# Side work moved to other units of a Fourier stage, and three output loads issued two units later, in a one-core kernel

## The chip, the cores and the metric

The kernel runs on one core of one Trainium2 chip. The metric is device time in microseconds (us) of one execution: the median of several runs.

## The reference

The inputs are `x` (2048 x 640), two pairs of Fourier matrices (real and imaginary, 2048 x 2048 and 640 x 640), `W_gate` and `W_up` (640 x 1728) and `W_down` (1728 x 640), all in fp32.

```python
xn   = layernorm(x)
a, b = xn @ hid_re.T, xn @ hid_im.T
y    = seq_re @ a - seq_im @ b                      # the Fourier mix
h    = relu(xn @ W_gate) * (xn @ W_up)
out  = x + y + h @ W_down
```

## The kernel before

Every matrix product is made in three matmuls of type fp32r (`mm3`, lines 129 to 131): each operand is split into a high and a low part, the high one by ScalarE (line 123), the low one by VectorE as the difference (line 124), and high x high, high x low and low x high are added up in PSUM. On top of that the 2 x 2 block products are made in Winograd's way, with seven products instead of eight, named B11, B21, T1, T2, B22, T3, T4. The T products need differences of blocks, which VectorE makes first (line 605 in the Fourier stage, 1060 in the last one).

Three stages follow each other.

1. The Fourier stage over the sequence. It runs over four chunks c of 512 output tokens. A chunk's products are cut into four units each (g = 0 to 3); a unit loads a 128 x 1024 tile of the Fourier matrix (`raw`, six buffers), splits it into a tile `cb` (a ring of three buffers) and runs 12 matmuls, or 18 for units of T1 and B22. A chunk from the second on is T1 x4, then T2 and B22 mixed, then T3 x4, then T4 x4. When a product's last unit is done, `combine` reads its sums out of PSUM with VectorE (lines 503, 506, 587).
2. The gate and up product (`gate_up`), first for the second pair of chunks (q = 1: tokens 1024 to 2047), then for the first.
3. The last stage (`project`), for q = 1 and then q = 0: it multiplies the Fourier result by the hidden Fourier matrices and `h` by `W_down`, seven products of six units each.

Stages 1 and 3 are written as a list `todo` of units, each with a load, a prepare, a run and a finish step. `drive(4, 2)` walks through the list: at place i it issues the load of unit i, the splits of unit i - 2, the matmuls of unit i - 4 and the finish of unit i - 5. In stage 1 this is the program's order, which a scheduler still changes by its own estimates; in stage 3 it holds as written on SyncE's and GpSimd's queues (SP and POOL).

Two kinds of side work stand in the list.

- Token steps: stage 2 needs blocks of normalized, transposed tokens of pair q = 1, with sums of them. Six steps (`token_sets`) make them. The first two (light) take two VectorE operations of 128 x 512 (lines 359, 360). The other four (heavy) take four of 128 x 512 (lines 378, 379) and four of 128 x 256 (line 385). Such a step is a list entry with no matmul of its own: at its place it loads `st` tiles (a pool of two buffers) from POOL's queue, six places later its VectorE work is made, and eight places later its stores to `set` are issued from POOL's queue. Chunk 3 then loads the nine finished sets on SP's queue (`K` and `A`, line 679) and splits them (`r` and `xs_early`).
- Loads of `y`: the output tiles begin as a piece of x, loaded on SP's queue (`get_y`, line 1161) after the fourth unit of a product, and the product's sums are added to them at its end (line 1164).

In the list before, the entry V3 stands at place 43. A token step is placed two entries after it, and each further one at least nine entries after the one before:

```python
            if n == "V3":
                free[0] = len(todo) + 2
            if free[0] is not None and len(todo) >= free[0] and steps:
                token_sets(*steps.pop(0))
                free[0] = len(todo) + SPACE
```

The loads of stage 3 are `rw` (data, line 1019 from the Fourier stage, 1021 from the stage of the gate) and `wr` (weights, lines 1050 to 1054); their splits are `cb` and `wt`.

Of the kernel before, what the change touches and what calls it, by code (L numbers as in the profile page):

```python
# [35 lines left out]
B11, B12, B21, B22, T1, T2, T3, T4, X4 = range(9)  # L36
# [22 lines left out]
def fnet_reglu_kernel(  # L59
# [84 lines left out]
    todo = []  # L144
# [270 lines left out]
    def sums_124(g):  # L415


        def make():
            both = lambda g, cs: [xn_block(g, cs, v) for v in range(2)]
            a11, a21, a12, a22 = both(g, K1), both(g, K2), both(g + NH, K1), both(g + NH, K2)  # L420
            s1, s2 = (i.rearrange("p (j d) -> p j d", j=SG) for i in (lambda t: (t[:, :CH], t[:, CH:]))(stage()))
            w = s4_part(g)
            tt = nc.vector.tensor_tensor
            f = lambda i: i.bitcast(F32)
            tc.keep_in_program_order(tt(s1, f(a21[0]), f(a22[0]), op=OP.add))
            tt(s1, s1, f(a22[1]), op=OP.add)
            tt(s2, s1, f(a11[0]), op=OP.subtract)
            tt(s2, s2, f(a11[1]), op=OP.subtract)
            split(*a21, s1)

            tt(s1, f(a12[0]), s2, op=OP.subtract)
            tt(s1, s1, f(a12[1]), op=OP.add)
            split(*a11, s2)
            split(w[:, :, 0], w[:, :, 1], s1)

        todo.append((idle, make, idle, idle))

    def sums_3(g):


        def make():
            s = stage()[:, :CH].rearrange("p (j d) -> p j d", j=SG)
            tt = nc.vector.tensor_tensor
            a22, s2 = ([xn_block(n, cs, v).bitcast(F32) for v in range(2)] for n, cs in ((g + NH, K2), (g, K1)))
            tc.keep_in_program_order(tt(s, a22[0], s2[0], op=OP.subtract))
            tt(s, s, a22[1], op=OP.add)
            tt(s, s, s2[1], op=OP.subtract)
            split(xn_block(g + NH, K1, 0), xn_block(g + NH, K1, 1), s)

        todo.append((idle, make, idle, idle))  # L450
# [220 lines left out]
    def load_set(q, blocks, get=stage):  # L671
        t = {}

        def load():
            if "sets_b" not in late:
                late["sets_b"] = {1: get_r1(F32R)}
            for i in blocks:
                t[i] = get()
                nc.sync.dma_start(t[i], sets[q][i])

        def prepare():
            for i in blocks:
                split(*set_parts(q, i), t[i])

        return load, prepare, idle, idle
# [15 lines left out]

    steps = [(q, i) for q in (1,) for i in range(SET_STEPS)]
    early_sets, first_sets = list(SETS_A), list(SETS_B)
    free, splits = [None], []
    SPACE = 9

    def phase(c, names):


        for n in names.split():  # L710
            if n == "K":
                later = load_set(1, [first_sets.pop(0)])
                todo.append((later[0], idle, idle, idle))
                splits.append((idle, later[1], idle, idle))
            elif n == "A":
                later = load_set(1, [early_sets.pop(0)])
                todo.append((later[0], idle, idle, idle))
                splits.append((idle, later[1], idle, idle))
            elif n == "s":
                todo.append(splits.pop(0))  # L720
            elif n[0] == "W":
                sums_124(int(n[1]))
            elif n[0] == "V":
                sums_3(int(n[1]))
            elif n[0] == "B" and n[2] == "1":
                first_stream(int(n[3]), n[:3], int(n[4]))
            else:
                stream(c, n[:-1], int(n[-1]))
            if n == "V3":
                free[0] = len(todo) + 2  # L730
            if free[0] is not None and len(todo) >= free[0] and steps:
                token_sets(*steps.pop(0))
                free[0] = len(todo) + SPACE

    for n in ("B11", "B21"):
        for g in range(NH):
            phase(0, f"{n}0{g} {n}1{g}")
    phase(0, "B1120 B1130 B1121 B1131 W0 B1122 B1132 B1123 W1 B1133 B2120 B2130 W2 B2121 B2131 B2122 V0 W3 B2132 B2123 B2133")
    phase(0, "V1 T10 T11 V2 T12 T13 V3 T20 B220 T21 B221 T22 T23 B222 B223 T30 T31 T32 T33 T40 T41 T42 T43")
    for c in range(1, NCHUNK - 1):  # L740
        phase(c, "T10 T11 T12 T13 T20 B220 T21 B221 T22 T23 B222 B223 T30 T31 T32 T33 T40 T41 T42 T43")
# [267 lines left out]
    def project(q):  # L1009
# [135 lines left out]
        def plain_run(tiles):  # L1145
            for key, e, c in tiles:
                new = key not in B
                if new:
                    B[key] = bank()
                cs, es = slice(c * CH, (c + 1) * CH), slice(PLACE[e] * P, (PLACE[e] + 1) * P)  # L1150
                (w, wr), (h, hr) = (PW["w"], PW["wr"]), (plain["h"], plain["hr"])
                mm3(B[key], (w[:, 0, es], w[:, 1, es]), (h[:, 0, cs], h[:, 1, cs]), new, False, not new)
                for v in range(2):
                    nc.tensor.matmul(B[key], wr[:, v, es], hr[:, cs], start=False, stop=v == 1, skip_group_check=not new)  # L1154

        def get_y(name):

            for e, c in {"B11": ((0, 0), (1, 0), (4, 1)), "T1": ((2, 1), (3, 1)), "B21": ((4, 0),),
                         "T2": ((0, 1), (1, 1)), "T4": ((2, 0), (3, 0))}.get(name, ()):
                y[e, c] = t = pool("y").tile([P, CH], F32, name=f"y{e}{c}")  # L1160
                nc.sync.dma_start(t, xt[e * P : (e + 1) * P, (c0 + c) * CH : (c0 + c + 1) * CH])  # L1161
# [28 lines left out]
        def read(name):  # L1190
            for r in reading(name):
                add_y(*r)

        for name in ("B11", "T1", "B21", "T2", "B22", "T3", "T4"):

            tiles = {"B21": [(("c", i), i, 0) for i in range(2)] + [("v1", 4, 0)],
                     "B22": [(("b", i), i, 1) for i in range(2)] + [("v2", 4, 1)],
                     "T3": [(("o", i), 2 + i, 1) for i in range(2)]}.get(name)
            for u in range(len(units)):
                l, p, r = unit(name, u, u == 0)  # L1200
                end = u == len(units) - 1 and not (tiles and name != "T3")
                todo.append((l, p, r, (lambda name: lambda: read(name))(name) if end else idle))
                if u == 3:
                    todo.append(((lambda name: lambda: get_y(name))(name), idle, idle, idle))
                if name == "B21" and u in (0, 2):
                    (plain_rest if u else plain_block)()
            if tiles:
                todo.append((idle, idle, (lambda t: lambda: plain_run(t))(tiles),
                             (lambda n: lambda: read(n))("own" if name == "T3" else name)))
            if name == "T3":  # L1210
                todo.append((idle, idle, lambda: plain_run([(("a", i), 2 + i, 0) for i in range(2)]), idle))

    PW, PARTS = {}, {"T2": Z2, "T3": Z3, "T4": Y22}
    for q in (1, 0):
        project(q)
# [41 lines left out]
```

## Time and profile before

| | us |
|---|---|
| median of 3 runs | 1036.84 |
| lowest, highest of them | 1034.75, 1037.27 |
| time of the profiled execution | 1032.92 |
| its span, first to last instruction | 1031.2 |
| TensorE (PE) busy | 1022.8 |
| VectorE (DVE) busy | 800.9 |
| ScalarE (ACT) busy | 433.3 |
| GpSimd (POOL) busy | 96.6 |

The profile is one execution; times in it count from its first instruction. A row of the timeline gives start, duration, engine, line, operation, output<-inputs, shape and count, and in brackets the idle time before it with what ended that. Matmul durations overlap, so for PE the distance from start to start is what counts. A row of the windows gives a stretch, its length, and then for PE, PEld (weight loads), DVE, ACT and POOL the busy time and the number of instructions; after them the granted clock, the share of the DMA engines' time and GB/s.

### The profile page before, as it was taken

The numbers are of one execution on the slowest core, as the hardware profiler recorded it, in microseconds if no ns is written. First come the engines' busy times: TensorE is split into PE (matmuls) and PEld (weight loads), VectorE is DVE, ScalarE is ACT, GpSimd is POOL, SyncE is SP. The second block draws the span as 40 slices with busy tenths as digits, with TensorE's granted clock in tenths as the row PEclk, the third lists the DMA queues.
The fourth block names the chain that finished last, engine by engine and source line by source line (L and its number), as shares of the span: only waits on it lengthen the run. The fifth ranks groups of instructions, "written<-read, shape, count | busy, mean of one in ns | idle before, by whom it ended". The sixth has DMA issues, their size and how long they took to land.

```text
span 1031.2 us, 12409 instructions
## 1 busy us (share of the span) xinstructions
PE 1022.8 (99%) x4528; PEld 844.3 (82%) x4528; DVE 800.9 (78%) x1072; ACT 433.3 (42%) x543; POOL 96.6 (9%) x161
## 2 busy tenths in 40 slices
PE   8999999999999999999999999999999999999998
PEld 7888888888888888888888888888888888888886
DVE  7947986978979897688878988886597667886764
ACT  6754443333333543333335443443355423552531
POOL 2000010101211001321110000000000000000000
PEclk9999999999999999999999999999999999999999
DMA  7975744957968864863364665654599647986543
GB/s 301 370 241 163 259 157 143 312 209 254 326 195 298 314 206 153 273 227 133 142 250 143 225 235 215 226 224 156 178 350 296 193 129 225 373 304 222 156 153 122
DMA packets 100156, 233.29 MB, mean 226 GB/s; under 512 B 11392, under 2 KB 50816, under 8 KB 98688
## 3 DMA queue, kind: packets, MB, share of 16 engines
q1 hardware_dynamic: 83088, 163.82, 47.4%
q0 software_dynamic: 17008, 68.69, 18.4%
q8 instruction: 35, 0.57, 0.2%
q14 instruction: 25, 0.20, 0.1%
HBM read 177.41 MB, written 54.02 MB: 224 GB/s over the span
## 4 chain that ended last, share of the span: by engine, by line
PE 96%; DVE 2%; issue 1%; DMA 1%; POOL 0%; SPq 0%; ACT 0%; POOLq 0%; DVEq 0%; ACTq 0%
PE ps L131 31%; PE ps L130 31%; PE ps L129 31%; PE ps L1154 1%; DMA rw<-hd 1%; DVE cb L124 0%; PE ps L493 0%; PE ps L465 0%; POOL cb L289 0%; DVE tk L605 0%; DVE raw L605 0%; DVE st L385 0%; DVE st L378 0%; SPq L1161 0%; DVE st L379 0%
## 5 line engine op out<-in xcount | busy, mean ns | idle before, releaser
L131 PE MATMUL ps<-cb,wt 128*128 128x512 f32 x390 | 151.9, 390 | 0.4 <-DVE wt L124 0.4
L129 PE MATMUL ps<-cb,wt 128*128 128x512 f32 x390 | 151.9, 390 | 0.0
L130 PE MATMUL ps<-cb,wt 128*128 128x512 f32 x390 | 151.8, 389 | 0.0
L124 DVE TENSOR_TENSOR cb<-rw,cb 128x1024 fp32r<-128x1024 f32 x83 | 94.0, 1133 | 68.6 <-ACT cb L123 67.9
L123 ACT ACTIVATE cb<-rw 128x1024 fp32r<-128x1024 f32 x83 | 82.0, 987 | 147.9 <-PE ps L131 127.2
L123 ACT ACTIVATE cb<-raw 128x1024 fp32r<-128x1024 f32 x78 | 82.5, 1059 | 123.5 <-PE ps L131 101.8
L124 DVE TENSOR_TENSOR cb<-raw,cb 128x1024 fp32r<-128x1024 f32 x78 | 95.2, 1221 | 38.9 <-ACT cb L123 38.6
L131 PE MATMUL ps<-xs_early,gw 128*128 128x512 f32 x260 | 101.2, 389 | 0.0
L130 PE MATMUL ps<-xs_early,gw 128*128 128x512 f32 x260 | 101.2, 389 | 0.0
L129 PE MATMUL ps<-xs_early,gw 128*128 128x512 f32 x260 | 101.1, 389 | 0.0
L130 PE MATMUL ps<-cb,xs_late 128*128 128x512 f32 x256 | 99.7, 390 | 0.1
L131 PE MATMUL ps<-cb,xs_late 128*128 128x512 f32 x256 | 99.6, 389 | 0.0
L129 PE MATMUL ps<-cb,xs_late 128*128 128x512 f32 x256 | 99.4, 389 | 0.0
L130 PE MATMUL ps<-cb,xs_early 128*128 128x512 f32 x238 | 92.7, 389 | 0.0
L131 PE MATMUL ps<-cb,xs_early 128*128 128x512 f32 x238 | 92.4, 389 | 0.0
L129 PE MATMUL ps<-cb,xs_early 128*128 128x512 f32 x238 | 92.2, 390 | 0.0
L120 ACT ACTIVATE gw<-z 128x1024 fp32r<-128x1024 f32 (+1 forms) x52 | 57.7, 1110 | 79.3 <-DVE z L776 73.7
L131 PEld LDWEIGHTS ps<-cb,wt 128*128 128x128 f32 x390 | 73.2, 188 | 15.9 <-DVE wt L124 0.7
L130 PEld LDWEIGHTS ps<-cb,wt 128*128 128x128 f32 x390 | 73.2, 188 | 15.7 <-DVE cb L124 0.3
L129 PEld LDWEIGHTS ps<-cb,wt 128*128 128x128 f32 x390 | 73.2, 188 | 15.4 <-ACT wt L123 0.2
L120 ACT ACTIVATE u<-ps 128x512 f32<-128x512 f32 x52 | 31.1, 598 | 96.4 <-PE ps L131 96.4
L786 DVE TENSOR_TENSOR gw<-z,gw 128x1024 fp32r<-128x1024 f32 (+1 forms) x52 | 64.7, 1285 | 2.2 <-ACT gw L120 2.2
(195 smaller groups left out, 1924.7 us busy)
## 6 DMA issues: line engine op xcount, KB each, us to landing
raw<-in_dft SPq DMA_DIRECT2D x94, 512.0 KB, 5.3
wt<-wparts SPq DMA_DIRECT2D x66, 256.0 KB, 3.2
z<-in_wgu SPq DMA_DIRECT2D x26, 640.0 KB, 4.0
hd<-ob POOLq DMA_DIRECT2D x26, 512.0 KB, 3.5
rw<-hd SPq DMA_DIRECT2D x24, 512.0 KB, 6.3
wparts<-pw POOLq DMA_DIRECT2D x11, 1024.0 KB, 4.1
tk<-in_dft SPq DMA_DIRECT2D x16, 512.0 KB, 7.4
rw<-pq SPq DMA_DIRECT2D x16, 512.0 KB, 7.6
```

The costliest lines, as they stand in the source:

```text
L120: return nc.scalar.activation(o, i, AF.Copy)
L123: nc.scalar.activation(hi, src, AF.Copy)
L124: return nc.vector.tensor_tensor(lo, src, hi.bitcast(F32), op=OP.subtract)
L129: nc.tensor.matmul(ps, wh, mh, start=first, stop=False, skip_group_check=more)
L130: nc.tensor.matmul(ps, wh, ml, start=False, stop=False, skip_group_check=more)
L131: nc.tensor.matmul(ps, wl, mh, start=False, stop=last, skip_group_check=more)
L786: tt(self.w[:, 1, cs], self.z[:, cs], self.w[:, 0, cs].bitcast(F32), op=OP.subtract)
L1154: nc.tensor.matmul(B[key], wr[:, v, es], hr[:, cs], start=False, stop=v == 1, skip_group_check=not new)
```

## The change

Token steps get fixed places in the list, and the loads of `y` for the first product of the last stage's first pair (q = 1, B11) are put into the list after that product's sixth unit instead of after the fourth. Nothing is added or removed.

```diff
-    free, splits = [None], []
-    SPACE = 9
+    splits = []
+
+    SET_UNITS = (46, 54, 62, 70, 83, 91)
...
-            if n == "V3":
-                free[0] = len(todo) + 2
-            if free[0] is not None and len(todo) >= free[0] and steps:
+            if steps and len(todo) >= SET_UNITS[-len(steps)]:
                 token_sets(*steps.pop(0))
-                free[0] = len(todo) + SPACE
...
-                if u == 3:
+                if u == (5 if (q, name) == (1, "B11") else 3):
                     todo.append(((lambda name: lambda: get_y(name))(name), idle, idle, idle))
```

Places of the six steps in the list, with the unit whose splits stand beside each step's VectorE work (six places later; cN is the chunk):

| step | place before | beside | place after | beside |
|---|---|---|---|---|
| 0, light | 46 | c0 T2 g3 | 46 | c0 T2 g3 |
| 1, light | 56 | c0 T4 g2 | 54 | c0 T4 g0 |
| 2, heavy | 66 | c1 B22 g1 | 62 | c1 T1 g3 |
| 3, heavy | 76 | c1 T4 g0 | 70 | c1 B22 g2 |
| 4, heavy | 86 | c2 B22 g0 | 83 | c2 T1 g2 |
| 5, heavy | 96 | c2 T3 g2 | 91 | c2 T2 g3 |

## The prediction

> **What bounds the kernel now.** I read the page's first part, then the windows by chunk, the PE timeline wherever a matmul started late, and the queue around those places.
>
> ```profile
> span 1031.2 us, 12409 instructions
> ## 1 busy us (share of the span) xinstructions
> PE 1022.8 (99%) x4528; PEld 844.3 (82%) x4528; DVE 800.9 (78%) x1072; ACT 433.3 (42%) x543; POOL 96.6 (9%) x161
> ```
>
> PE is the bound: outside its busy time there are 8.4 us, most of them the unchanged beginning and end. The change touches no matmul, so all that it can win is PE's waiting, and all that it can lose is new waiting. The two built programs have the same instructions, and the gate stage's order is the same; what differs lies in chunks 0 to 3 of the Fourier stage and in the last stage's first units. First the stretches from chunk 1's T1 to chunk 2's end, columns as for all windows (length, PE, PEld, DVE, ACT, POOL, clock, DMA share, GB/s):
>
> ```profile
> 204.00:226.30 22.30, 22.30 (x100) 18.49 (x99) 15.72 (x17) 7.57 (x8) 2.26 (x4) 1.00 0.62 234
> 226.30:247.00 20.70, 20.70 (x93) 17.14 (x92) 16.52 (x20) 6.37 (x6) 4.42 (x6) 1.00 0.60 203
> 247.00:269.00 22.00, 21.87 (x96) 17.65 (x95) 21.64 (x28) 8.51 (x8) 3.51 (x6) 1.00 0.94 306
> 269.00:290.00 21.00, 21.00 (x95) 17.36 (x94) 19.45 (x23) 7.05 (x8) 4.47 (x7) 1.00 0.81 285
> 290.00:313.00 23.00, 23.00 (x103) 19.07 (x102) 15.24 (x16) 6.89 (x7) 3.65 (x5) 1.00 0.60 202
> 313.00:336.00 23.00, 23.00 (x102) 18.99 (x102) 23.00 (x29) 8.50 (x8) 3.18 (x5) 1.00 0.90 328
> ```
>
> In the two T3/T4 stretches (third and sixth row) DVE has no time left: 21.64 of 22.00 and 23.00 of 23.00 us. In the other rows it idles 1.6 to 7.8 us. Heavy steps 3 and 5 lie in just these two. PE's one loss there is at the turn from chunk 1 to 2:
>
> ```profile
> 266.96 0.61 PE L129 MATMUL ps<-cb,xs_late 128*128 128x512 f32 x2
> 267.41 0.96 PE L129 MATMUL ps<-cb,xs_early 128*128 128x512 f32 x3
> 268.50 0.50 PE L130 MATMUL ps<-cb,xs_late 128*128 128x512 f32 x1
> 268.84 0.39 PE L131 MATMUL ps<-cb,xs_late 128*128 128x512 f32 x1
> 269.07 0.40 PE L129 MATMUL ps<-cb,xs_late 128*128 128x512 f32 x1
> ```
>
> ```profile
> PEld ps L130 <- DVE cb L124: 0.6, 1, 0.6
> ```
>
> Two matmuls take 0.45 us (266.96 to 267.41), so 0.225 each; a unit of 12 is 2.7 us, one of 18 is 4.1. The three at 267.41 belong to chunk 2: the scheduler had put them between those of chunk 1's last unit, and still PE waited for the low part of that unit's `cb`, as the second fence (waits in 246 to 270) says. From 267.41 to 268.84 four matmuls took 1.43 us against 0.90: 0.53 lost.
>
> The other loss is where the last stage begins:
>
> ```profile
> 747.25 0.48 PE L129 MATMUL ps<-cb,wt 128*128 128x512 f32 x1
> 747.76 0.50 PE L130 MATMUL ps<-cb,wt 128*128 128x512 f32 x1
> 748.63 0.50 PE L131 MATMUL ps<-cb,wt 128*128 128x512 f32 x1 [0.37 <-DVE wt L124]
> 748.97 0.40 PE L129 MATMUL ps<-cb,wt 128*128 128x512 f32 x1
> ```
>
> Three matmuls took 1.72 us against 0.68: 1.04 lost. This is B11's fifth unit (u = 4), and the queue tells why:
>
> ```profile
> 726.53 0.47 SPq L1050 DMA_DIRECT2D wr<-in_wd  x1
> 737.24 1.30 SPq L1161 DMA_DIRECT2D y<-in_xt  x3
> 738.58 0.90 SPq L1021 DMA_DIRECT2D rw<-hd  x1
> 739.53 0.47 SPq L1050 DMA_DIRECT2D wr<-in_wd  x1
> ```
>
> ```profile
> 745.39 1.06 ACT L123 ACTIVATE cb<-rw 128x1024 fp32r<-128x1024 f32 x1 [7.57 <-DMA rw<-hd]
> ```
>
> SP issued the fourth unit's loads by 727.00, then nothing for 10.2 us: the three `y` loads wait for PE's last matmul of the gate stage, whose memory they take, and the fifth unit's loads stand behind them. These came at 738.58, and ACT sat 7.57 us until the data was there.
>
> **The change part by part.** *The loads of y.* In the changed order the fifth unit's `rw` follows the fourth unit's `wr` directly, with no wait for an engine, and its `wr` with none but a landed transfer. So they go out at about 727 and, with even 7.5 us to land, are there at 735. What is late next is the buffer: `cb` is a ring of three and the first unit comes ready from elsewhere, so the fifth waits for the second unit's matmuls. Back from 747.25 lie the fourth (4.1), the third (a single block, 2.0) and then the second's end, at 741.1. With ACT's 1.06 and about 2 us of DVE after that, the splits end near 744.5, 2.7 us before 747.25. The whole 1.04 goes. The sixth unit's `wr` waits for the second unit's weights to be split, which is over by 737.0, where PE starts on that unit (741.1 less 4.1), and only `y` and what follows it is queued behind. The `y` loads go out at about the same 737.3 as before, since their own wait is what ended last; the next `rw` on SP moves from behind the two units' loads to behind `y`, earlier by about what those took. `y` is read at the end of B11, after 751.3 (748.63 plus twelve matmuls); even with 7.5 us to land it is there at 746. Cost nothing; gain 1.04. Bounds: 0, if another load is as late, and what the unprofiled runs lose there (below).
>
> *The heavy steps.* DVE's work of step 3 in the T4 of chunk 1:
>
> ```profile
> 253.12 0.69 DVE L378 TENSOR_TENSOR st<-st 128x512 f32<-128x512 f32 x1
> 253.73 1.22 DVE L605 TENSOR_TENSOR raw<-raw,tk 128x1024 f32<-128x1024 f32 x1
> 254.86 0.68 DVE L379 TENSOR_TENSOR st<-st 128x512 f32<-128x512 f32 x1
> 255.46 0.69 DVE L378 TENSOR_TENSOR st<-st 128x512 f32<-128x512 f32 x1
> 256.06 1.22 DVE L124 TENSOR_TENSOR cb<-raw,cb 128x1024 fp32r<-128x1024 f32 x1
> 257.20 0.68 DVE L379 TENSOR_TENSOR st<-st 128x512 f32<-128x512 f32 x1
> 257.80 1.09 DVE L385 TENSOR_TENSOR st<-st 128x256 f32<-128x256 f32 x3
> 258.81 1.22 DVE L124 TENSOR_TENSOR cb<-raw,cb 128x1024 fp32r<-128x1024 f32 x1
> 259.94 0.42 DVE L385 TENSOR_TENSOR st<-st 128x256 f32<-128x256 f32 x1
> 260.28 1.22 DVE L124 TENSOR_TENSOR cb<-raw,cb 128x1024 fp32r<-128x1024 f32 x1
> ```
>
> Start to start: 0.61 + 0.60 + 0.60 + 0.60 for the four, 1.01 + 0.34 for the rest, 3.8 us; a subtraction or a low part takes 1.14. The third window loses 3.8 us of DVE, so chunk 1's last low part comes over 3 us earlier, PE is not late at 268.50, and the built program runs those three matmuls in plain order. Gain 0.53, bounds 0 and 0.53. Step 3 goes to the turn from T2 to B22, step 5 likewise in chunk 2: the second and fifth rows, which have 4.2 and 7.8 us of idle DVE. Steps 2 and 4 go into T1, the first and fourth rows, with 6.6 us idle and 1.6, the latter with step 4 in it already. In all of these a unit of 18 matmuls gives DVE 4.1 us for 1.1 to 2.3 of its own. Cost 0 there. The light step moves by two units inside T4 of chunk 0: 1.2 us, as before.
>
> Each step's POOL work moves too. Heavy steps now follow each other after 8, 13 and 8 entries, where it was 10. Between two of them two stores must land and four loads follow. Eight entries here are seven units, some 24 us, less the step itself. A step that comes late blocks DVE in order, and behind it stand the low parts of the next units; but two or three finished units (8 us or more) lie before PE then. Taken as 0, up to 2.
>
> *What the scheduler moved with it.* Since step 5 ends earlier, the built program has the first two set loads of chunk 3 (`K`, 512 KB each) on SP directly behind T4 g1's load of chunk 2, and their splits in chunk 2's T3/T4, ACT's high parts both ahead of that of T3 g2. DVE there loses 3.8 us of step 5 and gets two low parts, 2.3: still 1.5 us less than the sixth row. Whether ACT waits hangs on the transfers; two DMA views, of 295 to 318 and of 320 to 340 (issuer, count, KB, median us to landing):
>
> ```profile
> raw<-in_dft SPq DMA_DIRECT2D x4, 512.0 KB, 3.3
> ...
> set<-st POOLq DMA_DIRECT2D x1, 512.0 KB, 3.9
> ```
>
> ```profile
> st<-set SPq DMA_DIRECT2D x2, 512.0 KB, 9.0
> set<-st POOLq DMA_DIRECT2D x1, 512.0 KB, 6.4
> ```
>
> Count from the end of T2 g1's matmuls in chunk 2. B22 g1, T2 g2, T2 g3, B22 g2 and g3 end at 4.1, 6.8, 9.5, 13.6 and 17.7, T3 g0 and g1 at 20.4 and 23.1. Step 5 starts when T2 g2 is split, just after 0, and with 3.8 us of its own and two operations of 1.14 between it ends at about 6.4. Its last store leaves at about 7 and lands at 11 (3.9); the two `K` loads leave at about 11.5 and land by 15 (3.3); ACT is done with both at 17.1. T3 g2's high part cannot start before 17.7 (ring). Nothing is lost in the calm stretch, which it is: 0.60 of the DMA share in the fifth row.
>
> *Sum.* 0.53 + 1.04 = 1.57 us off the profiled execution's 1032.92: 1031.35. The median of the runs shown stands 3.92 us above that execution; the same taken off it gives 1036.84 - 1.57 = 1035.27, say 1035.3, 0.15% faster. I take 0.3% (3.1 us) as what a measurement can tell from no change.
>
> **The rivals.** *Hidden stalls (faster).* The runs shown take 1.83 to 4.35 us more than the profiled one and spread by 2.5. The matmuls are the same, so some of this may be waiting that the profiled run did not have, and the two thin places are where it would sit: DVE at 23.00 of 23.00, and a load that ACT awaits for 7.57 us, of which every further microsecond goes to PE. If all 3.92 sit there, the time is 1036.84 - 1.57 - 3.92 = 1031.35; with half or more, about 1033.3 or less. It decides from 1.5 us of hidden waiting on. Against it: the surplus may lie in the ends of the span. 0.32.
>
> *Blocked set loads (slower).* If chunk 2's stretch is as busy as the second DMA view, the store lands at 13.4, the `K` loads leave by 14 and land at about 23 (9.0); ACT is done with them at 25, T3 g2's high part at 26, its low part at 27.1, while PE wants it at 23.3: 3.8 us lost. Behind it DVE has the two extra low parts, and by the same steps T3 g3 is 0.9 and T4 g1 0.5 late: 5.2 in all, 1035.3 + 5.2 = 1040.5. It costs PE from where the second `K` lands after 20, 5 us later than the calm rows say. For it: such loads took 9.0 when chunk 3's T1 loads stood beside them. Against it: those come later now. 0.13.
> [...]
> [...]
>
> *Nothing won.* The scheduler's other moves make another low part late by as much, or the fifth unit waits for another transfer: 1036.8. 0.05.
>
> **How the numbers follow.** The forecast, both small losses gone and no new one, has 0.50, with 1034.5 to 1036.3. Faster by over 0.3% is the first rival, 0.32; slower the second, 0.13; within it the forecast and the last, 0.55. The range reaches to 1032.0, which leaves out a quarter of the first rival (0.08), and to 1038.6, which holds the milder half of the second and leaves out 0.07: with the forecast's tails not quite 0.2.
>
> **What would show it.** Right: in chunk 1's and chunk 2's T3/T4 DVE's busy time falls by 3 to 4 and by about 1.5 us; PE has no start over 0.3 us apart near the turn to chunk 2; the fifth unit's `rw` is issued near 727, ahead of `y`, and PE has no gap in B11. Wrong: ACT waiting in T3 of chunk 2 for `st<-set` with PE late behind it; DVE waiting at line 378; `rw` of the fifth unit still waiting on SP; or a profile as forecast with a time that does not follow.

## The result and the profile after

| | before | after |
|---|---|---|
| median, us | 1033.98 | 1032.02 |
| lowest, highest, us | 1031.51, 1037.62 | 1030.75, 1033.83 |
| standard deviation, us | 1.57 | 0.74 |
| profiled execution, us | 1032.92 | 1030.75 |

There are 22 runs of each. The ratio of after to before is 0.9981, with a 95% interval of 0.9974 to 0.9987: 0.2% faster, less than the 0.3% that the prediction took as its bound for a difference. The median of before, 1036.84 when the prediction was made, stands for three runs; over 22 runs it is 1033.98.

The first part of the page of after:

```profile
span 1029.0 us, 12406 instructions
## 1 busy us (share of the span) xinstructions
PE 1022.7 (99%) x4528; PEld 845.6 (82%) x4528; DVE 800.8 (78%) x1072; ACT 433.0 (42%) x543; POOL 96.6 (9%) x161
```

No engine works less; only the span is shorter, by 2.2 us. PE's 1022.7 us of work now leave 6.3 us instead of 8.4.

**The turn to chunk 2.** The timeline of PE in after, at the start of chunk 1's last unit, where before lost 0.53 us, and at its end:

```profile
266.50 0.39 PE L129 MATMUL ps<-cb,xs_late 128*128 128x512 f32 x1
266.73 0.39 PE L130 MATMUL ps<-cb,xs_late 128*128 128x512 f32 x1
...
269.00 0.39 PE L131 MATMUL ps<-cb,xs_late 128*128 128x512 f32 x1
269.23 0.39 PE L129 MATMUL ps<-cb,xs_early 128*128 128x512 f32 x1
```

The matmuls start 0.22 to 0.23 us apart, and the first `xs_early` of chunk 2 comes after the whole of that unit, not in the middle of it. The windows of after, for chunk 1's T3/T4, chunk 2's first half and chunk 2's T3/T4 (columns as in the prediction):

```profile
247.00:269.00 22.00, 22.00 (x99) 18.21 (x97) 19.85 (x21) 8.50 (x8) 3.84 (x6) 1.00 0.96 343
...
290.00:313.00 23.00, 23.00 (x104) 19.02 (x103) 19.12 (x24) 7.08 (x7) 1.80 (x3) 1.00 0.52 189
313.00:336.00 23.00, 23.00 (x103) 19.01 (x102) 21.54 (x23) 11.40 (x12) 1.39 (x3) 1.00 0.99 369
```

DVE is relieved in both T3/T4 stretches, from 21.64 to 19.85 and from 23.00 to 21.54, and the second row carries step 5 now (15.24 before).

**The last stage.** The timeline of SP's queue in after, and then PE's at the unit that was late before:

```profile
725.99 0.47 SPq L1019 DMA_DIRECT2D rw<-hd  x1
726.50 0.47 SPq L1048 DMA_DIRECT2D wr<-in_wd  x1
727.06 0.43 SPq L1019 DMA_DIRECT2D rw<-hd  x1
735.56 0.37 SPq L1048 DMA_DIRECT2D wr<-in_wd  x1
736.16 1.35 SPq L1159 DMA_DIRECT2D y<-in_xt  x3
```

```profile
746.17 0.39 PE L129 MATMUL ps<-cb,wt 128*128 128x512 f32 x1
746.40 0.39 PE L130 MATMUL ps<-cb,wt 128*128 128x512 f32 x1
746.62 0.39 PE L131 MATMUL ps<-cb,wt 128*128 128x512 f32 x1
```

The fifth unit's loads are the rows at 725.99 and 726.50, the sixth's those at 727.06 and 735.56. In before the fifth's `rw` stood at 738.58, behind `y`. The loads of `y` now leave last, at 736.16, and PE runs through. (After's clock is 1.06 us ahead of before's here: the fourth unit's `rw` leaves at 725.06 against 726.12.)

Where the profiled executions differ: each stretch's loss is what the distances between matmul starts exceed 0.2275 us, summed. In the Fourier chunks (204 to 402) it went from 0.56 to 0, in B11 (725 to 760) from 1.31 to 0.21. That makes 1.66 of the 2.17 us. The other 0.5 us lies at the very start, where PE's Fourier products begin 0.4 us earlier; that start moves from execution to execution (11.8 to 13.0 us in the profiled executions of before). PE, DVE and ACT have the same work in the same order in both kernels until 187 us, so this 0.5 us is not put down to the change.

### The profile page after: what moved, and what is told of

The parts are those of the page before. It is cut to its first block, busy times and chain, and to the rows that moved or that the text cites. A ratio compares the mean times of both kernels' runs of the same rounds, so it can differ in the third digit from the quotient of the medians.

```text
span 1029.0 us, 12406 instructions
## 1 busy us (share of the span) xinstructions
PE 1022.7 (99%) x4528; PEld 845.6 (82%) x4528; DVE 800.8 (78%) x1072; ACT 433.0 (42%) x543; POOL 96.6 (9%) x161
## 4 chain that ended last, share of the span: by engine, by line
PE 98%; issue 1%; POOL 0%; DVE 0%; POOLq 0%
PE ps L131 32%; PE ps L130 32%; PE ps L129 32%; PE ps L1152 1%; PE ps L493 0%; PE ps L465 0%; POOL cb L289 0%; DVE y L1162 0%; POOL mv L292 0%; POOLq L289 0%; POOLq L292 0%; POOLq L1248 0%
```

## The experiments

Every kernel was compared with the kernel before on the same chip. Each diff is against the kernel named with it.

**The loads of y alone** (against before):

```diff
-                if u == 3:
+                if u == (5 if (q, name) == (1, "B11") else 3):
```

> Token steps as before, only the y loads of B11 two units later. Own theory (two small losses that add up): the loss of 1.04 us in B11's fifth unit is gone, its rw issued near 727, while the one of 0.53 us at the turn from chunk 1 to 2 stays with the three matmuls of chunk 2 put in between; about 1.0 us off the time, ratio to before 0.9990. Rival (one part carries all of it, because the unprofiled runs wait far longer for this load than the profiled one): 0.9981 or less here and nothing left for the steps.

Measured: 1032.12 us against 1033.64, ratio 0.9985 (0.9972 to 0.9998). The loss in B11 went from 1.31 to 0.19 us; that at the turn stays, 0.53. The time can't tell own theory (0.9990) from rival (0.9981): both lie in the interval. The runs spread as before's do (standard deviation 1.61 us, against 1.66 for before beside them). Another 0.5 us is lost in chunk 3, as PE's timeline of this kernel shows:

```profile
361.35 0.39 PE L129 MATMUL ps<-cb,gw 128*128 128x512 f32 x1
361.90 0.50 PE L130 MATMUL ps<-cb,gw 128*128 128x512 f32 x1 [0.16 <-DVE cb L124]
```

The second waits for a low part that DVE makes late. One of three further profiled executions of before loses 0.67 us at the same place (below), so this is before's own weakness, which shows in some executions.

**The token steps alone** (against after):

```diff
-                if u == (5 if (q, name) == (1, "B11") else 3):
+                if u == 3:
```

> Token steps moved, y loads where they were. Own theory: PE has no late start at the turn to chunk 2 (0.53 us won), and B11's fifth unit still starts about 1.0 us late behind a load issued near 738; ratio to before 0.9995. Rival (the steps carry it, by waiting in the T3/T4 stretches that the profiled run of before did not show): 0.9985 or less here.

Measured: 1032.06 us, ratio 0.9982 (0.9971 to 0.9992), standard deviation 0.70. The turn's loss is gone. B11's stays, and the timelines of SP's queue and of PE in this kernel show both ends of it:

```profile
737.41 1.30 SPq L1159 DMA_DIRECT2D y<-in_xt  x3
738.75 0.43 SPq L1019 DMA_DIRECT2D rw<-hd  x1
...
747.73 0.40 PE L130 MATMUL ps<-cb,wt 128*128 128x512 f32 x1
748.50 0.50 PE L131 MATMUL ps<-cb,wt 128*128 128x512 f32 x1 [0.37 <-DVE wt L124]
```

With `y` ahead of `rw`, the matmul at 748.50 is 0.54 us late again. The Fourier chunks lose 0.52 us in all, 0.4 of it at one matmul of chunk 2's T4 (333.13) that waits for a low part; after's profiled execution has no such loss, though its smallest margin, 0.2 us, is in the same product. So each part removes the loss that it was said to remove, and leaves the other's. The times of the two kernels (1.5 and 1.6 us below before) do not add up to the whole's 1.96, but their intervals are as wide as the parts themselves; it is the places of the losses that tell the parts apart. The time of this kernel is what the rival foresaw (0.9985 or less); the 0.9995 of own theory lies outside the interval. So the steps save more in the runs than the 0.53 us at the turn, and the profiled execution, slower than most of the twelve, does not show where.

**The loads of y one unit earlier than before** (against after), a dose in the other direction:

```diff
-                if u == (5 if (q, name) == (1, "B11") else 3):
+                if u == (2 if (q, name) == (1, "B11") else 3):
```

> As changed, but the y loads after B11's third unit, so that the loads of the fourth unit too stand behind them on SP. Own theory (what costs is the place on SP's queue, since the y loads wait there for the gate stage's last matmul): the fourth unit's rw is issued near 738 instead of 727 and its last split ends near 748.6 on the clock of before, where PE wants it at 743.7: about 5 us lost there, the fifth unit then hardly late; time 5 us over the changed kernel's, ratio to before about 1.003. Rival (what cost was the traffic of 768 KB beside the rw loads, wherever it stands): about 1 us lost as in before, ratio about 0.9995.

Measured: 1038.29 us, ratio 1.0041 (1.0026 to 1.0056). B11 loses 6.24 us instead of 0.21, somewhat more than expected. SP's queue and PE in this kernel, and then its windows:

```profile
736.06 1.28 SPq L1159 DMA_DIRECT2D y<-in_xt  x3
737.38 0.43 SPq L1019 DMA_DIRECT2D rw<-hd  x1
...
741.76 0.39 PE L131 MATMUL ps<-cb,wt 128*128 128x512 f32 x1
745.52 0.49 PE L129 MATMUL ps<-cb,wt 128*128 128x512 f32 x1 [3.37 <-ACT wt L123]
...
747.43 0.63 PE L129 MATMUL ps<-cb,wt 128*128 128x512 f32 x1
747.86 0.63 PE L130 MATMUL ps<-cb,wt 128*128 128x512 f32 x1
```

```profile
742.00:745.50 3.50, 0.14 (x1) 0.00 (x0) 0.81 (x1) 1.86 (x2) 0.00 (x0) 1.00 1.04 383
745.50:748.00 2.50, 2.11 (x5) 1.34 (x6) 2.21 (x3) 1.80 (x2) 0.00 (x0) 0.75 1.06 409
748.00:750.00 2.00, 2.00 (x7) 1.52 (x6) 1.85 (x3) 1.77 (x2) 0.00 (x0) 0.50 1.06 394
```

`y` leaves at 736.06, close to the 736.16 of after, since its own wait ends it; here it is the fourth unit's `rw` that stands behind it, one unit nearer to its use. PE waits 3.5 us for it (741.76 to 745.52 less one distance). What follows has a price of its own: the granted clock falls to 0.50, the starts stand 0.43 us apart (747.43 to 747.86) until 749.99, and this takes about 1.6 us. The rival, that the traffic of `y` is what costs, does not hold: the fourth unit's `rw` took 6.2 us to land right behind `y`, and in after, ahead of `y`, the fifth's took 7.1 and the sixth's 9.4. It is the place on the queue, in both directions.

**The loads of y one unit later instead of two** (against after):

```diff
-                if u == (5 if (q, name) == (1, "B11") else 3):
+                if u == (4 if (q, name) == (1, "B11") else 3):
```

> As changed, but the y loads after B11's fifth unit: one unit later than before instead of two, so that the sixth unit's loads stand behind them. Own theory: the sixth unit is wanted at 751.3 and its loads from 738.6 are split by 749, so nothing is lost; ratio to before 0.9981, same as changed. Rival (both units are needed, since the sixth unit's loads land late too): 0.5 to 1.5 us lost in B11's sixth unit, ratio 0.9990.

Measured: 1031.94 us, ratio 0.9976 (0.9965 to 0.9987); B11 loses 0.19 us. SP's queue in this kernel:

```profile
726.38 0.47 SPq L1019 DMA_DIRECT2D rw<-hd  x1
...
736.55 1.29 SPq L1159 DMA_DIRECT2D y<-in_xt  x3
737.94 0.38 SPq L1019 DMA_DIRECT2D rw<-hd  x1
```

Only the fifth unit's load has to go ahead of `y`. The sixth's may stand behind it, at 737.94, and is still in time.

**Step 3 back, and steps 4 and 5 one place later** (against after):

```diff
-    SET_UNITS = (46, 54, 62, 70, 83, 91)
+    SET_UNITS = (46, 54, 62, 76, 84, 92)
```

> As changed, but heavy step 3 at place 76 again, beside T4 of chunk 1 (steps 4 and 5 one place later, 84 and 92, since steps must stand 8 apart). Own theory (a heavy step in T3/T4 leaves VectorE no time, and costs little in a calm run, more in others): the loss of about 0.5 us at the turn to chunk 2 is back, and the runs spread as wide as those of before (standard deviation 1.5 us or more); median 0.5 to 1 us over the changed kernel, ratio to before 0.9987. Rival (the wide spread of before comes from step 5 or from the late set loads, not from step 3): spread 0.5 to 0.8 us as with all steps moved, ratio 0.998.

Measured: 1040.47 us, ratio 1.0060 (1.0039 to 1.0080), far from what was expected. The 0.53 us at the turn came back. But PE lost 0.9 us near 305 and 4.8 us between 319 and 326, and these two rows of the kernel's timeline show at what:

```profile
301.89 0.69 DVE L378 TENSOR_TENSOR st<-st 128x512 f32<-128x512 f32 x1 [3.76 <-DMA st<-in_xt]
...
319.89 1.06 ACT L123 ACTIVATE r<-st 128x1024 fp32r<-128x1024 f32 x1 [6.11 <-DMA st<-set]
```

Step 5 stood in DVE's queue before its token loads had landed, and ACT waited 6.11 us for a set load with a high part that PE needed behind it. One place for steps 4 and 5 weighs more than ten times what step 3 does, so this kernel says little of step 3; it raised the question of step 5's place, which the kernel with step 5 one place later answers.

**Step 5 back alone** (against after):

```diff
-    SET_UNITS = (46, 54, 62, 70, 83, 91)
+    SET_UNITS = (46, 54, 62, 70, 83, 96)
```

> As changed, but heavy step 5 at place 96 again, beside T3 of chunk 2, so that the set loads come late in chunk 3 again too. Own theory: no loss in the profile, since before had none there either, but margins under 0.5 us in chunk 2's T4; if step 5 makes the wide spread of before, the standard deviation is 1.5 us or more here and the ratio 0.999; otherwise (step 3 makes it) 0.5 to 0.8 us and 0.998.

Measured: 1031.42 us, ratio 0.9975 (0.9963 to 0.9987), standard deviation 0.62. Nothing is lost anywhere in the Fourier chunks or B11 (0.03 and 0.23 us), with DVE full again in chunk 2's T3/T4, by the window of this kernel:

```profile
313.00:336.00 23.00, 23.00 (x103) 19.02 (x102) 23.00 (x28) 8.50 (x8) 3.18 (x5) 1.00 0.91 331
```

A full DVE costs nothing here as long as its order suits PE. Moving step 5 brings nothing. This is the fastest median of all kernels that ran, but its interval and that of after overlap.

**Steps 4 and 5 late, 2 and 3 as before** (against after):

```diff
-    SET_UNITS = (46, 54, 62, 70, 83, 91)
+    SET_UNITS = (46, 56, 66, 76, 92, 100)
```

> Token steps later than before, at places 46, 56, 66, 76, 92, 100, so that two heavy steps fall on chunk 2's T3/T4 (beside B22 g3 and T4 g2) and step 5 runs into chunk 3's set loads. Own theory: VectorE, at 23.00 of 23.00 us there with one step, lacks about 2 to 3 us; PE loses 1.5 to 4 us late in chunk 2 or early in chunk 3, ratio to before 1.001 to 1.003. Rival (the steps' place hardly matters, since finished units lie ahead of PE): loss under 0.5 us, ratio 0.9985 to 0.9995 from the y loads alone.

Measured: 1041.12 us, ratio 1.0062 (1.0047 to 1.0078); the Fourier chunks lose 9.29 us. Both expectations were missed, and own theory's reason, a VectorE without time left, as well. The waits from 313 to 360, and then the window of chunk 2's T3/T4:

```profile
ACT r L123 <- DMA st<-set: 9.2, 3, 5.7
...
DVE st L378 <- DMA st<-in_xt: 5.0, 1, 5.0
```

```profile
313.00:336.00 23.00, 20.34 (x85) 16.41 (x84) 17.92 (x24) 5.31 (x5) 4.41 (x7) 0.93 0.87 305
```

PE is starved there while DVE is busy only 17.92 of 23 us. The price of a misplaced step here is not DVE's load. It is an engine that stands in its own order and waits for a transfer, once DVE for token loads (5.0 us) and three times ACT for set loads (9.2).

**Step 3 alone, the rest as before** (against before, which has places 46, 56, 66, 76, 86, 96; written as fixed places):

```diff
+    SET_UNITS = (46, 56, 62, 70, 86, 96)
```

> Of the token steps only the heavy steps 2 and 3 are moved (places 46, 56, 62, 70, 86, 96; step 3 out of chunk 1's T4), y loads where they were. Own theory (step 3's place alone makes the loss at the turn to chunk 2 and the wide spread of before's runs): no late start at that turn, about 1.0 us still lost in B11's fifth unit, standard deviation 0.5 to 0.8 us and a ratio to before of 0.998, as with all steps moved. Rival (the spread comes from steps 1, 4 or 5 or from the start): standard deviation 1.5 us or more, ratio 0.9995.

Measured: 1033.26 us, ratio 0.9994 (0.9985 to 1.0002), standard deviation 0.97. The turn's loss is gone (0.01 us in the Fourier chunks), but the time is not clearly shorter. Its profiled execution, 1034.03 us, loses 2.12 us in B11, where `y` is as before, and 1.3 us at 33 us. Step 2 had to move with step 3 (66 to 62). The spread, 0.97, lies between what own theory and rival expected (before had 1.22 beside these runs), and the time of 0.998 was missed; the profiled execution shows one reason, B11, and what the other runs lost it cannot tell.

**Step 5 one place later** (against after):

```diff
-    SET_UNITS = (46, 54, 62, 70, 83, 91)
+    SET_UNITS = (46, 54, 62, 70, 83, 92)
```

> As changed, but step 5 one place later: 92 instead of 91. The first set loads and their splits stay ahead of chunk 2's T3 g2 to g3 in the queues. Own theory (set loads block ScalarE, and the changed kernel is a few us from it): the second store leaves about 4 us later, the first set load lands about 317 to 319 where ScalarE has it ahead of T3 g2's high part, and PE loses 2 to 5 us in chunk 2's T3; median 3 to 7 us over the changed kernel, ratio to before 1.001 to 1.005. Rival (what cost 6 us with step 3 back was the short distance of steps 4 and 5 to each other, eight places, whose token loads came late): loss under 1 us, ratio 0.998 to 0.999.

Measured: 1034.57 us, ratio 1.0000 (0.9989 to 1.0011): the whole gain is gone, and 6.2 us are lost in chunk 2's T3 in the profiled execution (1036.75 us). Its timeline (POOL, SP's queue, ACT, PE) and one window:

```profile
307.44 0.77 POOL L394 DMA_DIRECT2D set<-st  x1 [4.11 <-DVE cb L124]
...
313.85 0.98 SPq L679 DMA_DIRECT2D st<-set  x2
...
317.71 0.39 PE L131 MATMUL ps<-cb,xs_late 128*128 128x512 f32 x1
318.37 1.06 ACT L123 ACTIVATE r<-st 128x1024 fp32r<-128x1024 f32 x1 [8.64 <-DMA st<-set]
319.33 1.04 ACT L123 ACTIVATE cb<-raw 128x1024 fp32r<-128x1024 f32 x1
320.42 0.79 PE L129 MATMUL ps<-cb,xs_late 128*128 128x512 f32 x1 [2.32 <-ACT cb L123]
321.68 0.79 PE L130 MATMUL ps<-cb,xs_late 128*128 128x512 f32 x1 [0.47 <-DVE cb L124]
```

```profile
322.00:324.00 2.00, 2.00 (x6) 1.52 (x6) 2.00 (x3) 1.21 (x2) 0.00 (x0) 0.50 0.76 281
```

The chain can be read from row to row. The last store leaves at 307.44 (302.57 in after); the set loads wait for it and leave at 313.85 (308.91 in after); ACT, which has the first set's split ahead of T3 g2's high part, waits 8.64 us and makes that high part 0.96 us after; PE waits 2.71 us from start to start and then runs at a granted clock of 0.50 (322 to 324), its matmuls 0.43 us apart until 326.97. This is the prediction's slower rival, one place away from the kernel that was measured. The profiled execution is the slowest of twelve, though: the others go down to 1031.69, the median is 2.5 us above after's, and the 1.001 to 1.005 expected was missed. The rival of this run, a loss under 1 us, fails in the trace.

**The kernel before, profiled again three times.** There is no edit; the question is what its waits cost from one execution to the next.

> The kernel before again, one look, to see where one more execution of it waits. Own theory: the same two places as in the first profile (0.5 us at the turn to chunk 2, 1.0 us in B11's fifth unit), and in a longer execution more of the first, in T3/T4 of chunks 1 or 2. Rival: a longer execution has its surplus at the start, ahead of 15 us, where the change does nothing.

> The kernel before, another look. Own theory: about 0.55 us lost at the turn to chunk 2 and 1.0 in B11's fifth unit; if this execution is over 1034, its surplus is in chunk 1's or 2's T3/T4. Rival: the surplus is ahead of 45 us.

> The kernel before, a third look, for the same reason: own theory and rival as for the second.

Measured: 1032.87, 1034.98 and 1033.67 us. The turn costs the same each time (0.53 us). B11 loses 1.18, 1.81 and 1.74 us, against 1.31 in the first profile. The second of these, on ACT and PE:

```profile
747.48 1.06 ACT L123 ACTIVATE cb<-rw 128x1024 fp32r<-128x1024 f32 x1 [8.10 <-DMA rw<-hd]
748.55 0.39 PE L131 MATMUL ps<-cb,wt 128*128 128x512 f32 x1
749.33 0.50 PE L129 MATMUL ps<-cb,wt 128*128 128x512 f32 x1 [0.39 <-ACT wt L123]
```

ACT waits 8.10 us here instead of 7.57, and PE is late at the first matmul of the unit already, not only from its second on. In the second execution there is also 0.67 us at 362 us, in chunk 3; and from 11 to 45 us the three lose 1.2 to 1.6 us, against 0.93 in the first profile. The surplus of that execution, 1034.98 us, was thus not in T3/T4 of chunks 1 and 2, where it was expected, but spread over the start, chunk 3 and B11.

## Why the prediction was right

It foresaw 0.15% off the time, both small losses gone and no new one, and 0.19% was measured (0.13 to 0.26). By its steps:

- *The loads of y*: right. On the clock of before it had the fifth unit's `rw` leave at about 727, `y` at about 737.3 and the fifth unit's splits end near 744.5. With 1.06 us added to after's times these are 727.05, 737.2 and 744.5. The bound of 7.5 us for a landing was too low, 9.4 for the sixth unit's `rw`, but ACT waited for PE there and not for the load. The experiments show that one unit would do, and that an earlier `y` costs 6 us; so the queue is the cause, shown in both directions.
- *The heavy steps, 0.53 us*: right in size and cause. The turn's loss is gone in each kernel with step 3 at place 70, and is there, 0.53 us, in each with it at 76, also where step 2 had moved (step 3 back, with step 2 at 62). The relief of DVE in chunk 1's T3/T4 was overstated: the trace shows 1.8 us, not 3 to 4, since work of chunk 2 that waited before moved up into that stretch. In chunk 2's T3/T4 it is 1.5, as forecast, but it bought nothing: with step 5 left in place PE loses nothing either. The order after has a thin place of its own in chunk 2's T4, 0.2 us wide in its trace, where the steps-alone kernel lost 0.4; the prediction had such a place only in its last rival.
- *Eight entries, "0, up to 2"*: 0 in after. The margin is visible: step 5 starts without a wait at 294.83 (below), about 2 us after its loads have landed. Where steps 4 and 5 came one place later it was 3.76 us of DVE and 0.9 of PE, and 5.0 us of DVE where they came nine places late; the bound held for this kernel's places only.
- *The set loads, "nothing is lost in the calm stretch"*: right in the outcome, wrong in the size. These rows of after's timeline tell it (the prediction's clock has its zero near 294.3):

```profile
294.83 0.69 DVE L378 TENSOR_TENSOR st<-st 128x512 f32<-128x512 f32 x1
...
302.57 0.77 POOL L394 DMA_DIRECT2D set<-st  x1 [2.71 <-DVE cb L124]
308.91 0.80 SPq L679 DMA_DIRECT2D st<-set  x2
312.29 1.06 ACT L123 ACTIVATE r<-st 128x1024 fp32r<-128x1024 f32 x1 [2.31 <-DMA st<-set]
313.52 1.06 ACT L123 ACTIVATE r<-st 128x1024 fp32r<-128x1024 f32 x1 [0.18 <-DMA st<-set]
314.49 1.04 ACT L123 ACTIVATE cb<-raw 128x1024 fp32r<-128x1024 f32 x1
```

The last store left at 8.3 on that clock, not 7, the two loads at 14.6, not 11.5, and the second was split from 19.2, where 15 had been said and 20 was the point from which PE pays. The store was the term that was mis-sized. Among after's transfers from 302.5 to 309 it took 6.2 us from issue to landing, where a row of before gave 3.9:

```profile
set<-st POOLq DMA_DIRECT2D x1, 512.0 KB, 6.2
```

Four of the five microseconds of margin were gone. The low part that PE needs of that unit ended 1.6 us before its matmul. The chance of 0.13 for this rival was thus for a place that had hardly a microsecond to spare, and the kernel one place later pays it, by the chain that the rival describes. The two loads, which SP issues, landed after 3.3 and 4.2 us, where the prediction had 3.3.

- *Hidden stalls*: part of it was there. Before's profiled executions lose 1.2 to 1.8 us in B11 and one of four loses 0.67 us in chunk 3; after's lost 0.21 and nothing. The spread fell from 1.57 to 0.74 us, and the medians differ by 1.96 us where the sum was 1.57. The spread went with the token steps and not with `y`: 0.70 with the steps alone, 1.61 with `y` alone. What the rival rested on, runs 1.83 to 4.35 us above the profiled one, was mostly the chance of three runs: over 22 runs the median of before is 1.06 us above its profiled execution, and that of after 1.27.
- *The time itself* came out 3.3 us under the forecast of 1035.3. Of this, 2.86 us is the median of before, 1036.84 in three runs and 1033.98 in 22. A forecast that is a difference from a median cannot be nearer than that median is. The measured 1032.02 lies outside the 1034.5 to 1036.3 of the forecast, among the times of the first rival, and only 0.02 us inside the stated range, whose lower end had been set for that rival. That it came to lie inside is luck; the change against before, 1.96 us where 1.57 was forecast, is not.

What stays open is what makes up the rest of before's spread, and by it where the steps alone save 1.6 us: the stretch from 11 to 45 us, the Fourier chunks and B11 together lose 2.8 to 4.3 us in its four profiled executions (1.2 in that of after), but the runs without a profile show no places. Nor is it settled why moving steps 2 and 3 alone narrowed it less than all of them did.

## What to carry to other kernels

On SP's queue here the loads of `y`, which waited 10.2 us in before, held up the loads behind them: the fifth unit's `rw` left at 738.58 behind them and, in after, at 725.99 ahead of them. Such a load belongs behind those that are needed sooner; one unit later was enough here, and two did no harm. When side work is moved, write down when its last store lands and which engine stands waiting for the reload with its next work behind it (ACT for 8.64 us with step 5 one place later), with the margin to the next operation that the bound engine needs: this kernel sits one list place from a loss of 6.2 us in a traced execution and 2.5 us in the median, and its own time shows nothing of it. Look for the gain by place in the trace, not in the time, where it is about as large as the spread of the runs.

## What the runs showed of the hardware

In some kernels that lost time the granted clock was lower behind a wait of PE, and the blocked queue cost more than the wait alone, by about 1.6 us in the first of them.

- With the early `y` loads PE idled 3.37 us ahead of the matmul at 745.52. The clock was 0.75 from 745.5 to 748 and 0.50 from 748 to 750 (windows above); the starts from 746.84 to 750.30 took about 1.6 us more than at 0.2275 us each.
- With step 5 one place later PE idled 2.32 us ahead of the matmul at 320.42, which took 0.79 instead of 0.39 us. The clock was 0.50 from 322 to 324 and 0.85 on average from 313 to 336.
- With step 3 back PE idled 2.15 us ahead of the matmul at 321.95. The clock was 0.65 from 322 to 324 and 0.93 on average from 313 to 336.
- With the steps late PE's longest wait between 313 and 360 was 2.7 us, and the clock was 0.93 on average from 313 to 336.
- In before PE idled 1.39 us ahead of the matmul at 6.58, and the clock was 1.00 from 6 to 12.

Each of these is one profiled execution. They do not show how long a wait has to be for this.
